# A narrow matmul tail cut into 32-column tiles, one row tile's statistics moved from VectorE to ScalarE, and the order of tasks retuned

## The chip, the cores and the metric

The kernel runs on one core of a Trainium2 chip. The metric is the device time of one execution in microseconds, the median of several. Each run is labelled fast or slow, from its time and its granted clock.

## The reference, cut to what matters

One transformer layer's work on x of 2048 rows by 512, in bf16: a layernorm, then attention and a gated feed-forward network on the same normalised rows, both added to x.

```python
xn = _layernorm(x, axis=-1)                      # mean, variance, eps 1e-5, no scale or bias
return x + _A_ref(xn, A_wqkv, A_wo) + _B_ref(xn, B_w_gate, B_w_up, B_w_down)
# _A_ref: 32 heads of 16; each row attends to 8 rows, 2 apart; softmax; output projection
# _B_ref: (gelu(xn @ w_gate) * (xn @ w_up)) @ w_down, inner width 1376
```

## The kernel before: the parts that the change touches

The program is a list of tasks with inputs, outputs, a cost and a priority. A list scheduler orders them for each of five engines, from the costs, the priorities and a table of corrections called SHIFT. Each engine's program is then its list in that order, with semaphore waits between engines. So a change of one task can move tasks elsewhere.

The inner width of 1376 is ten tiles of 128 and a rest of 96. The last 64 columns of w_up, "the up tail", have no full-width matmul to go with. They run at the head of the task that sums the attention logits, whose matmuls are 32 columns wide, four side by side on TensorE:

```python
for kt in range(4):
    for c in range(2):                                   # the up tail: two tiles of 64 columns
        ins = e.matmul(PS[64 * c:64 * c + 64, 512 * itu.slot:512 * itu.slot + 256],
                       lhsT=Wt[:, kt, 128:192],
                       rhs=xnT[:, itx.slot, kt, 256 * c:256 * c + 256],
                       start=(kt == 0), stop=(kt == 3), tile_position=(0, 64 * c))
for (g, prs) in grp:
    for wq in range(2):
        for sj in range(4):                              # the logits: four tiles of 32 columns
            ins = e.matmul(PS[32 * sj:32 * sj + 32, ...], lhsT=E8[:, 24 - 8 * g:56 - 8 * g], ...,
                           tile_position=(0, 32 * sj))
```

There are four such tasks, one per 512 rows. The attention output uses 32-wide matmuls too (weights E4). In two of the four places such an output block lies right before the task; so there are six narrow blocks in all.

The layernorm's statistics were made by VectorE for every row tile of 128 rows, and the start of the program has a fixed order on each engine ("chain"):

```python
t_of["bnst%d" % t] = G.task("dve", ..., lambda e: e.bn_stats(out=st[:, t, :], in_=XIN[:, it.slot, t2, :]), ...)
t_of["bnag%d" % t] = G.task("dve", ..., lambda e: e.bn_aggr(out=mv[:, t, :], in_=st[:, t, :]), ...)
# ... cut ...
chain(["bnst0", "bnag0", "sub0", "rstd0", "norm0", "bnst1", "bnag1", "evy0_0", "sub1", "rstd1", "norm1", ...
```

## Time and profile before

| | before |
|---|---|
| time, median of 6 runs | 195.23 us (195.07 to 195.54) |
| profiled span | 193.5 us |
| TensorE busy | 97% of the span |
| Q weights landed | 6.13 us |
| first projection on TensorE starts | 6.26 us |
| last matmul starts | 190.78 us |

The three views (the page's totals and chain, TensorE's waits, the timeline of one narrow block) are shown and read in the prediction. One more is needed to follow the second row tile. These are lines of the timeline of the kernel before; the columns are start and length in us, engine, line, operation, output and inputs, their sizes, the count, and in brackets the idle time before and what ended it:

```profile
4.75 0.69 DVE L937 BATCH_NORM_STATS2 st<-XIN 128x6 f32<-128x512 bf16 x1
...
5.38 0.38 ACT L1039 ACTIVATE xnT<-PS 128x256 bf16<-128x256 bf16 x1 [1.13 <-PE PS L1019]
...
6.21 0.35 DVE L993 TENSOR_SCALAR XIN<-XIN,rstd 128x512 bf16<-128x512 bf16 x1
...
6.26 0.61 PE L1077 MATMUL PS<-xnT,Wqkv 128*128 128x128 bf16 x8 [0.65 <-DVE rstd L969]
...
6.71 0.39 PE L1019 MATMUL PS<-ident,XIN 128*128 128x128 bf16 x4
```

VectorE takes the second tile's statistics at 4.75 and has it normalised at 6.56. ScalarE evacuates the first tile's transposes until 5.76. TensorE waits 0.65 us, then multiplies the first tile with the Q weights at 6.26, and turns to the second tile's transposes at 6.71, when that tile has been ready for 0.15 us.

### The profile page before, as it was taken

To read this page: it belongs to the slowest core of one execution; us is meant where nothing else is said; L and a number is where in the kernel's file an instruction comes from. 1 tells how busy PE (TensorE), PEld (TensorE's weight loads), DVE (VectorE), ACT (ScalarE), POOL (GpSimd) and SP (SyncE) were. 2 spreads that over 40 slices of the span, in tenths; PEclk is the share of its full clock that TensorE was granted. 3 is DMA by queue.
4 is the path that set the end of the run, shared out by engine and by line. 5 is a ranking of instruction groups with operands and counts; after the bars stand their busy time and mean duration, and the time that the engine had idled before them with its cause. 6 is when DMAs were issued, how large, how long until landed. Compare 5 with 4: busy or idle time off the path is not lost.

```text
span 193.5 us, 3221 instructions
## 1 busy us (share of the span) xinstructions
PE 187.4 (97%) x1207; PEld 91.6 (47%) x1224; DVE 153.2 (79%) x241; ACT 104.0 (54%) x171; POOL 16.2 (8%) x31
## 2 busy tenths in 40 slices
PE   6899999999999999999999999999999999999994
PEld 2794444444444444444444444444444444444484
DVE  5898999999998988995895699988997089931132
ACT  3587583996676665501667777328266640048000
POOL 6013001014711000000200000000000000000000
DMA  5999999898375006953511587420250298130121
GB/s 134 354 396 305 327 168 178 216 277 186 71 181 106 2 3 160 234 156 105 181 36 50 140 216 157 130 77 0 68 128 21 62 243 189 54 112 0 44 79 41
DMA packets 34800, 27.03 MB, mean 140 GB/s; under 512 B 11265, under 2 KB 33249, under 8 KB 34785
## 3 DMA queue, kind: packets, MB, share of 16 engines
q1 hardware_dynamic: 34784, 26.83, 54.6%
q8 instruction: 9, 0.15, 0.3%
q14 instruction: 7, 0.05, 0.1%
HBM read 19.99 MB, written 5.26 MB: 131 GB/s over the span
## 4 chain that ended last, share of the span: by engine, by line
PE 93%; ACT 2%; DVE 2%; DMA 1%; issue 1%; DVEq 0%
PE PS L1374 34%; PE PS L1453 20%; PE PS L1131 18%; PE PS L1449 7%; PE PS L1077 4%; PE PS L1342 4%; PE PS L1215 4%; PE PS L1409 1%; PE PS L1208 1%; DMA XIN<-in_A_x_dram 1%; ACT OT L1354 1%; DVE st L937 1%; PE PS L1019 0%; ACT UU L1391 0%; DVE XIN L976 0%
## 5 line engine op out<-in xcount | busy, mean ns | idle before, releaser
L1453 PE MATMUL PS<-Wd,HT 128*128 128x512 bf16 (+2 forms) x207 | 41.2, 345 | 0.1
L1374 PE MATMUL PS<-xnT,Wu 128*128 128x512 bf16 x157 | 39.9, 379 | 0.3 <-issue 0.2
L1374 PE MATMUL PS<-xnT,Wg 128*128 128x512 bf16 x154 | 39.3, 379 | 0.7 <-issue 0.5
L1185 DVE TENSOR_TENSOR UNI<-QT,KT 128x2048 bf16<-128x2048 bf16 x32 | 37.2, 1221 | 2.3 <-PE PS L1342 1.5
L1384 ACT ACTIVATE GG<-PS 128x512 bf16<-128x512 f32 x40 | 23.8, 601 | 26.5 <-PE PS L1374 23.1
L1131 PE MATMUL PS<-xnT,Wqkv 128*128 128x512 bf16 x156 | 34.8, 379 | 0.3 <-issue 0.2
L1391 ACT ACTIVATE UU<-PS 128x512 bf16<-128x512 f32 x40 | 24.0, 599 | 15.6 <-PE PS L1374 15.6
L1396 DVE TENSOR_TENSOR HT<-GG,UU 128x512 bf16<-128x512 bf16 x40 | 16.2, 418 | 17.3 <-ACT UU L1391 17.1
L1453 PEld LDWEIGHTS PS<-Wd,HT 128*128 128x128 bf16 x209 | 19.6, 98 | 18.6
L1374 PEld LDWEIGHTS PS<-xnT,Wg 128*128 128x128 bf16 x160 | 15.4, 98 | 19.4 <-issue 0.8
L1374 PEld LDWEIGHTS PS<-xnT,Wu 128*128 128x128 bf16 x160 | 15.5, 98 | 19.3 <-issue 0.8
L1131 PEld LDWEIGHTS PS<-xnT,Wqkv 128*128 128x128 bf16 x160 | 15.5, 98 | 18.8 <-ACT OT L1354 0.4
L1473 DVE TENSOR_TENSOR OB<-PS,XR 128x512 bf16<-128x512 f32 (+2 forms) x19 | 11.4, 602 | 11.8 <-PE PS L1453 11.6
L1322 DVE TENSOR_TENSOR UNI<-BS,PT 128x2048 bf16<-128x2048 bf16 x16 | 19.5, 1219 | 0.6 <-DMA PT<-pt_scratch 0.5
L1322 DVE TENSOR_TENSOR BS<-BS,PT 128x2048 bf16<-128x2048 bf16 x16 | 19.6, 1222 | 0.3
L1449 PE MATMUL PS<-Wo,OT 128*128 128x512 bf16 (+2 forms) x75 | 16.7, 345 | 0.1
L1148 ACT ACTIVATE KT<-PS 128x512 bf16<-128x512 f32 x12 | 7.3, 606 | 14.3 <-PE PS L1131 14.3
L1155 ACT ACTIVATE VT<-PS 128x512 bf16<-128x512 f32 x16 | 9.6, 597 | 4.4 <-PE PS L1131 4.4
L937 DVE BATCH_NORM_STATS2 st<-XIN 128x6 f32<-128x512 bf16 x16 | 10.7, 685 | 1.0 <-DMA XIN<-in_A_x_dram 1.0
L1171 POOL COPY KT<-KT 128x64 bf16<-128x64 bf16 x3 | 7.6, 2518 | 40.0 <-ACT KT L1148 38.6
L1354 ACT ACTIVATE OT<-PS 128x512 bf16<-128x512 f32 x16 | 8.3, 602 | 4.3 <-PE PS L1342 4.3
L1449 PEld LDWEIGHTS PS<-Wo,OT 128*128 128x128 bf16 x76 | 7.2, 98 | 7.0
(66 smaller groups left out, 150.3 us busy)
## 6 DMA issues: line engine op xcount, KB each, us to landing
BS<-vt_scratch SPq DMA_DIRECT2D x64, 128.5 KB, 3.5
vt_scratch<-VT SPq DMA_DIRECT2D x16, 128.0 KB
XR<-in_A_x_dram SPq DMA_DIRECT2D x16, 128.0 KB, 2.2
out_dram<-OB SPq DMA_DIRECT2D x14, 128.0 KB, 2.1
Wqkv<-in_A_wqkv_dram SPq DMA_DIRECT2D x3, 512.0 KB
XIN<-in_A_x_dram SPq DMA_DIRECT2D x6, 256.0 KB, 5.8
Wg<-in_B_w_gate_dram SPq DMA_DIRECT2D x1, 1280.0 KB
Wu<-in_B_w_up_dram SPq DMA_DIRECT2D x1, 1280.0 KB
```

Source lines behind the costliest of these rows:

```text
L937: return lambda e: e.bn_stats(out=st[:, t, :], in_=XIN[:, it.slot, t2, :])
L1131: ins = e.matmul(PS[:, 512 * it.slot:512 * it.slot + HWD], lhsT=lhsT, rhs=xnT[:, itx.slot, kt, c0:c0 + HWD], start=(kt == 0), stop=(kt == 3))
L1185: return lambda e: e.tensor_tensor(out=UNI[:, it.slot, :, :], in0=bass.AP(QT, (itq.slot * 4 + g) * 512, [[NQT * 4 * 512, 128], [0, 4], [1, ...
L1322: return lambda e: e.tensor_tensor(out=dst(), in0=bass.AP(BS, it.slot * 4 * 514 + o, [[NBS * 4 * 514, 128], [514, 4], [128, 4], [1, 128]]) ...
L1354: return lambda e: e.activation(out=OT[:, ito.slot, dq, :], in_=PS[:, 512 * it.slot:512 * it.slot + 512], func=ACTF.Identity)
L1374: ins = e.matmul(PS[0:M, 512 * it.slot:512 * it.slot + 512], lhsT=Wx[:, kt, j * 128:j * 128 + M], rhs=xnT[:, itx.slot, kt, :], start=(kt = ...
L1384: return lambda e: e.activation(out=GG[0:M, ito.slot, :], in_=PS[0:M, 512 * it.slot:512 * it.slot + 512], func=ACTF.Gelu_apprx_tanh)
L1391: return lambda e: e.activation(out=UU[0:M, ito.slot, :], in_=PS[0:M, 512 * it.slot:512 * it.slot + 512], func=ACTF.Identity)
L1396: return lambda e: e.tensor_tensor(out=HT[0:M, ito.slot, j, :], in0=GG[0:M, ig.slot, :], in1=UU[0:M, iu.slot, :], op=ALU.mult)
L1449: ins = e.matmul(PS[:, 512 * it.slot:512 * it.slot + CW], lhsT=OT[:, ito.slot, dq, ti * 128:(ti + 1) * 128], rhs=Wo[:, dq, c0:c1], start=( ...
L1453: ins = e.matmul(PS[:, 512 * it.slot:512 * it.slot + CW], lhsT=HT[:, ith.slot, j, ti * 128:(ti + 1) * 128], rhs=Wd[:, j, c0:c1], start=Fal ...
L1473: return lambda e: e.tensor_tensor(out=OB[:, ito.slot, 0:CW], in0=PS[:, 512 * it.slot:512 * it.slot + CW], in1=XR[:, itx.slot, c0:c1], op= ...
```

## The change

The intent of the three parts: fewer changes of matmul width on TensorE; VectorE relieved of one row tile's statistics at the crowded start; and the SHIFT table tuned again.

```diff
 SHIFT = {
-    "acc0": 223, "acc1": 3251, "er1": 857, "er2": 1563, "er3": -682, ...      # (cut: 5 lines)
+    "acc1": 4275, "er1": 814, "er2": 3235, "er3": -369, "fin0": 704, ...      # (cut: 4 lines)
 }
...
+                if t == 1:
+                    for (nm, dur, kw, rd, wr) in (
+                            ("sx1", 0.55, dict(out=junk[:, :], func=ACTF.Identity, accum_out=sums[:, 0:1]), ...),
+                            ("negm1", 0.2, dict(out=sums[:, 1:2], in_=sums[:, 0:1], func=ACTF.Identity,
+                                                scale=-1.0 / D), ...),
+                            ("sxx1", 0.55, dict(out=junk[:, :], func=ACTF.Square, bias=sums[:, 1:2],
+                                                accum_out=sums[:, 2:3]), ...),
+                            ("var1", 0.2, dict(out=mv[:, 1, 1:2], in_=sums[:, 2:3], func=ACTF.Identity,
+                                               scale=1.0 / D), ...)):
+                        ... # four ScalarE tasks
+                    t_of["mean1"] = G.task("dve", "mean1", 0.1, ...)           # mean = sum / D
+                    continue
...
-        chain(["bnst0", "bnag0", "sub0", "rstd0", "norm0", "bnst1", "bnag1", "evy0_0", "sub1", "rstd1", "norm1",
+        chain(["bnst0", "bnag0", "sub0", "rstd0", "norm0", "mean1", "sub1", "evy0_0", "rstd1", "norm1",
...
-                chain(["evx0_0", "sq1", "evx0_1", "evq0_0", "sq2"])
+                chain(["sx1", "sq0", "negm1", "sxx1", "var1", "sq1", "evx0_0", "evx0_1", "evq0_0", "sq2"])
...
-                            for c in range(2):
-                                ins = e.matmul(PS[64 * c:64 * c + 64, 512 * itu.slot:512 * itu.slot + 256],
-                                               lhsT=Wt[:, kt, 128:192],
-                                               rhs=xnT[:, itx.slot, kt, 256 * c:256 * c + 256],
-                                               start=(kt == 0), stop=(kt == 3), tile_position=(0, 64 * c))
+                            for c in range(4):
+                                ins = e.matmul(PS[32 * c:32 * c + 32, 512 * itu.slot:512 * itu.slot + 256],
+                                               lhsT=Wt[:, kt, 128 + 32 * (c % 2):160 + 32 * (c % 2)],
+                                               rhs=xnT[:, itx.slot, kt, 256 * (c // 2):256 * (c // 2) + 256],
+                                               start=(kt == 0), stop=(kt == 3), tile_position=(0, 32 * c))
```

## The prediction

> **What bounds the kernel now.** I read the page's first and fourth parts, then TensorE's own waits, then the timeline around one narrow-tile block, then the start of the chain.
>
> ```profile
> PE 187.4 (97%) x1207; PEld 91.6 (47%) x1224; DVE 153.2 (79%) x241; ACT 104.0 (54%) x171; POOL 16.2 (8%) x31
> ...
> PE 93%; ACT 2%; DVE 2%; DMA 1%; issue 1%; DVEq 0%
> ```
>
> TensorE is busy for 97% of the 193.5 us span, and 93% of the chain that ended last is TensorE. A busy matmul engine is not always a full one, so the next view lists everything TensorE waited for:
>
> ```profile
> PE PS L863 <- DVE wsrc L812: 1.5, 1, 1.5
> PE PS L1077 <- DVE rstd L969: 0.7, 1, 0.7
> PE PS L1374 <- issue: 0.6, 4, 0.2
> PE PS L1131 <- issue: 0.2, 1, 0.2
> ```
>
> The first two are before 6.26 us; after that nothing is waited for except "issue". I went through the starts of consecutive matmuls in the trace. A full 128x512 one follows the last at 0.2157 us without exception, but for two things: about a dozen steps of exactly twice that, which are lost records (17 of the full-width matmuls that the program has are missing from the trace, and a lost record after a narrow block also makes the "0.16 issue" below), and the changes of tile width. One real wait is left after 6.26: 0.19 us at 7.37, for the second row tile's evacuation. So from 6.26 to 191.04 TensorE is full, and the time moves only by (a) what TensorE itself has to do, (b) its start, (c) the 2.4 us tail, (d) stalls that a new order brings.
>
> For (a), the block in which the up tail lies:
>
> ```profile
> 72.79 0.39 PE L1342 MATMUL PS<-BS,E 128*32 128x512 bf16 x4
> 73.11 0.63 PE L1208 MATMUL PS<-xnT,Wt 128*64 128x256 bf16 x8
> 73.67 1.91 PE L1215 MATMUL PS<-UNI,E 128*32 128x512 bf16 x32
> 75.73 0.59 PE L1131 MATMUL PS<-xnT,Wqkv 128*128 128x512 bf16 x2 [0.16 <-issue]
> ```
>
> Columns: start, length, engine, line, tiles, weights' shape, moving shape, count. The four 32-wide matmuls at 72.79 stream together for 0.216, to 73.00; L1208 (the up tail) starts at 73.107, so going from 32-wide to 64-wide cost 0.103. Its pairs start at 73.107, 73.240, 73.350 and 73.459; the last ends streaming at 73.568, and L1215 starts at 73.665: going back to 32-wide cost 0.097. From full width to a narrow block (28.96 to 29.05) it is 0.093.
>
> For (b), the start of the chain:
>
> ```profile
> 4.83 0.61 DVE st L937
> 5.45 0.02 issue
> 5.47 0.18 DVE mv L941
> 5.65 0.18 DVE xnT L1031
> 5.83 0.26 DVE XIN L976
> 6.09 0.10 DVE rstd L969
> 6.19 0.07 issue
> 6.26 0.61 PE PS L1077 x8
> ```
>
> This reads as if VectorE's statistics of the second row tile (st, mv at 4.83 to 5.65) held the first projection. They do not. That matmul needs the first row tile's transposes, evacuated by 5.76 (ScalarE) and 5.83 (VectorE), and the Q weights. The trace's DMA completions put the last of the 16 pieces of those weights at 6.13, TensorE's semaphore wait for them ends at 6.155 to 6.206, and its weight load starts at 6.23. The chain names the reciprocal only because it is the nearest earlier end. The start is held by a 512 KB weight load which the change leaves alone.
>
> **What the Trainium skill says.** "TensorEngine Tiling (Array Packing)", Tiling Modes, Key Properties: changing the tiling mode, not just the tile, drains TensorE, and different tiles load weights and multiply in parallel. The trace agrees: 0.093 to 0.106 us at each change of width, and four 32-wide matmuls start within 0.01 us of each other. "TensorE: Matmul & The Clock Gate", section "Wait — 56ns, not 53.3ns?": start to start is N / 2.4 GHz plus 2.5 ns when warm, so 0.109 for N = 256; the 64-wide pairs show 0.109 to 0.110. "ScalarE: Activation LUTs", What ACT_TABLE_LOAD costs: an ACTIVATE takes 186 ns + 0.833 ns per element, 93 ns more with a bias pointer, and neighbours overlap by about 93 ns. Here the 512-wide copies take 597 ns (613 by the formula) and the one-column square root with a bias pointer 297 ns (281).
>
> **The change part by part.**
> *Up tail.* Eight 64-wide matmuls of 256 columns, in concurrent pairs, become sixteen 32-wide ones, in groups of four. Streaming is the same: four steps of 0.109. What goes is changes of width, as both neighbours that are narrow are 32-wide. The change to 32-wide after the up tail goes in all four blocks: 4 x 0.097 = 0.39. The change before it goes where another 32-wide block comes right before, two of four (the lists of both programs agree on that): 2 x 0.103 = 0.21. The first pair after a change takes 0.133 in place of 0.109; this 0.024 goes in two blocks for sure: 0.05. Sum 0.65 us, all on TensorE's full stretch, so all of it counts. I take 0.6, because groups of four must have four weight loads of 97 ns done within 109 ns, with little to spare.
>
> *Second row tile.* VectorE loses bn_stats 0.685 and its aggregation 0.18 and gains a one-column multiply, about 0.16. ScalarE gains two passes over 512 columns (estimated by the skill's formula at 0.61 and 0.71, the second having a bias pointer) and two one-column operations (0.19 each). In order: the row tile's DMA lands at 3.46; sum 3.49 to 4.10; first tile's square root 4.00 to 4.30 (was 3.95); negative mean 4.21 to 4.40; squares 4.42 to 5.13; variance 5.15 to 5.35; square root 5.37 to 5.67 (was 5.69 to 5.98); evacuation of the first transposes 5.57 to 5.96 (was 5.38 to 5.76). The second tile is normalised at about 6.3 instead of 6.56, but TensorE gets to its transposes only at 6.70, behind eight matmuls that wait for the weights: gain 0. The later evacuation at 5.96 is still ahead of 6.13: loss 0, with 0.15 us to spare.
>
> *The retuned priorities.* The diff replaces the whole table, and this is its largest part in the program. The lists show the same TensorE instructions in another order, with the same six narrow blocks, so no work is gained or lost; only stalls could come. I checked the tight places. The first logits block moves up: 56 full matmuls instead of 68 after 14.49, so 14.49 + 56 x 0.2157 = 26.6. Its eight VectorE products now run without a break from about 15.5, at a step of 1.135: 15.5 + 7 x 1.135 + 1.22 = 24.7, 1.9 us ahead. The fourth logits block keeps its distance (products end 124.89, block at 126.14 now). In the trace the last product of the four output blocks ends 1.0, 2.2, 2.0 and 3.8 us ahead of its block (70.26 before 71.27, and so on). In the new order, adding up streaming times, the first of them comes at about 72.9, 1.6 us later, with about as much VectorE work ahead of its last input (one 0.42 us product less, one 0.68 us product more). The third and fourth come about 1.5 us earlier, 0.65 of it the shift that I predict; the third has one 0.42 us product less in front of its last input, whose wait for a ScalarE copy (one per 1.73 us of matmuls) goes too; the fourth had 3.8 us. At the end there are five groups instead of four between the last narrow block and the final output tiles, which cover the four evacuations (2.0 us) at least as well. The final tiles and stores are unchanged: tail 0.
>
> Sum: 195.24 - 0.6 = 194.6 us; the span goes from 193.5 to about 192.9.
>
> **Rivals.** *The chain is right and the statistics hold the start:* then about 0.25 us more would come (6.56 to 6.3): 194.4. For it speaks only the chain; against it the landing at 6.13. *ScalarE becomes the bound at the start:* if accumulating costs ScalarE 0.1 us a pass more, the evacuation ends near 6.2, the first projection slips by 0.1 to 0.2, and, as TensorE is full afterwards, the slip stays: 194.8. Nothing in the trace has an accumulating pass, so this is open. *The new order stalls TensorE:* one late product or evacuation costs some tenths to 1 us: 195 to 195.6. For it: ScalarE and VectorE orders changed everywhere; and VectorE is 94 to 96% busy from 14.5 to 75.7 and from 111 to 129 us. Against: the old order, made by the same scheduler with the same margins, had no stall with a VectorE just as full. *Sixteen short weight loads do not keep up,* say 0.15 per group instead of 0.11: 4 x 4 x 0.04 = 0.64 lost, and the gain is gone: 195.2.
>
> **Range and chances.** The main term is six changes of width, each measured; the rivals lie mostly above. The runs of before span 0.47 us. Predicted 194.6, range 194.0 to 195.4. Two per cent is 3.9 us: a gain of that size is nowhere to be had with TensorE full (faster 0.01), a loss would need several long stalls (slower 0.02), so within 2% has 0.97.
>
> **What would show it.** Right: the up tail's line shows groups of four at 0.109 us, the next block starts without 0.1 us in between, the block at 73 lasts 0.2 us less, the first projection stays at 6.2 to 6.3, and TensorE waits for nothing new. Wrong: a first projection that moves with the statistics, up tail groups at clearly over 0.11, or a named wait of TensorE after 7.6 us.

## The result, and the profile after

The changed kernel takes 194.76 us (median of 6 fast runs, 194.5 to 195.03) against 195.23. The ratio is 0.9975, with a 95% interval of 0.9962 to 0.9988. Ratios here are the mean time of one kernel's fast runs over that of the other's of the same rounds, so they are not quite the ratio of the medians quoted. The gain of about a quarter of a per cent is real, as the interval leaves out 1.

First the page's totals and its chain, of the changed kernel:

```profile
PE 186.6 (97%) x1239; PEld 92.0 (48%) x1256; DVE 152.4 (79%) x240; ACT 106.1 (55%) x177; POOL 15.7 (8%) x31
...
PE 93%; DMA 4%; issue 1%; SPq 0%; DVE 0%; DVEq 0%
```

TensorE's share is as before. In the chain VectorE's share at the start has gone, and the load of the Q weights stands there (2.3% of the span). ScalarE's 2% of before were not at the start: they lay at 152.6 to 156.2, where TensorE had a lost record. An output store at the end makes up most of the rest of the 4% of DMA. TensorE's waits, of the changed kernel (what waited for what, us in total, times, longest):

```profile
PE PS L866 <- DVE wsrc L815: 1.5, 1, 1.5
PE PS L1098 <- DMA Wqkv<-in_A_wqkv_dram: 0.7, 1, 0.7
PE PS L1395 <- issue: 0.6, 4, 0.2
PE PS L1395 <- ACT OT L1375: 0.3, 2, 0.2
```

The same 0.7 us wait that was put down to VectorE's reciprocal before is now put down to the load of the Q weights. The third and fourth lines are not waits: each is a narrow block (the 32- and 64-column matmuls between two full-width ones) followed by a full-width group with one record lost, which the block below shows (x3 where the program has four). Here 17 of the 1256 matmuls have no record, as in the trace of the kernel before (1207 of 1224), while all weight loads have theirs.

Now the timeline of the block that the prediction showed for the kernel before, in the changed one:

```profile
74.42 0.39 PE L1363 MATMUL PS<-BS,E 128*32 128x512 bf16 x4
74.64 0.61 PE L1229 MATMUL PS<-xnT,Wt 128*32 128x256 bf16 x16
75.08 1.90 PE L1236 MATMUL PS<-UNI,E 128*32 128x512 bf16 x32
77.13 0.81 PE L1395 MATMUL PS<-xnT,Wu 128*128 128x512 bf16 x3 [0.16 <-ACT OT L1375]
```

From the last output group to the up tail it is 0.22 us, which is just the group's streaming; it was 0.32. From the up tail to the logits it is 0.44, four steps of 0.11; it was 0.56. Two changes of width and the slow first pair have gone.

Last, the start in the changed kernel, the answer to the timeline shown of the kernel before:

```profile
3.40 0.63 ACT L952 ACTIVATE junk<-XIN 128x512 bf16<-128x512 bf16 x1 [1.11 <-DMA XIN<-in_A_x_dram]
...
3.93 0.19 ACT L952 ACTIVATION_READ_ACCUMULATOR junk<-XIN 128x1 f32 x1
...
4.43 0.72 ACT L952 ACTIVATE junk<-XIN,sums 128x512 bf16<-128x512 bf16 x1
...
5.06 0.19 ACT L952 ACTIVATION_READ_ACCUMULATOR junk<-XIN,sums 128x1 f32 x1
...
5.28 0.35 DVE L997 TENSOR_SCALAR XIN<-XIN,mv 128x512 bf16<-128x512 bf16 x1 [0.32 <-ACT junk L952]
...
5.72 0.36 ACT L1060 ACTIVATE xnT<-PS 128x256 bf16<-128x256 bf16 x1
...
6.04 0.35 DVE L1014 TENSOR_SCALAR XIN<-XIN,rstd 128x512 bf16<-128x512 bf16 x1
...
6.29 0.61 PE L1098 MATMUL PS<-xnT,Wqkv 128*128 128x128 bf16 x8 [0.67 <-DMA Wqkv<-in_A_wqkv_dram]
```

The second tile is normalised at 6.40 instead of 6.56. The first tile's evacuation ends at 6.08 instead of 5.76, behind the passes on ScalarE. The Q weights land at 6.15, and the first projection starts at 6.29, which is 0.03 us later than before. Two instructions that the program does not name, the reads of the accumulator, come with the two passes.

To separate start and rest I use one mark in all kernels below, the *gate*: the start of the first matmul of the second row tile's Q projection, where TensorE waits for an evacuation for the last time. From there to the start of the last matmul is the *body*.

| profiled run | gate | last matmul starts | body |
|---|---|---|---|
| before | 7.57 | 190.78 | 183.21 |
| changed | 7.60 | 190.10 | 182.50 |

The body is 0.71 us shorter; the gate is 0.03 us later; the tail after the last matmul's start is 2.7 us in both (193.5 - 190.78 and 192.8 - 190.10). All six narrow blocks account for the 0.71, measured from the end of streaming of the last full-width matmul to the first full-width matmul after the block (where that one's record is lost, its start is taken as the next one's less a step of 0.216):

| block | before | changed | difference |
|---|---|---|---|
| logits 0 alone | 2.50 | 2.38 | -0.12 |
| outputs 0 and logits 1 | 4.35 | 4.11 | -0.24 |
| outputs 1 and logits 2 | 4.35 | 4.11 | -0.24 |
| logits 3 alone | 2.51 | 2.38 | -0.12 |
| outputs 2, outputs 3 | | | 0 |

### The profile page after: what moved, and what is told of

It reads as the page before. It is cut to its first block, busy times and chain, and to the rows that moved or that the text cites. A ratio compares the mean times of both kernels' runs of the same rounds, so it can differ in the third digit from the quotient of the medians.

```text
span 192.8 us, 3283 instructions
## 1 busy us (share of the span) xinstructions
PE 186.6 (97%) x1239; PEld 92.0 (48%) x1256; DVE 152.4 (79%) x240; ACT 106.1 (55%) x177; POOL 15.7 (8%) x31
## 4 chain that ended last, share of the span: by engine, by line
PE 93%; DMA 4%; issue 1%; SPq 0%; DVE 0%; DVEq 0%
PE PS L1395 36%; PE PS L1474 18%; PE PS L1152 18%; PE PS L1470 7%; PE PS L1098 4%; PE PS L1363 4%; PE PS L1236 4%; DMA Wqkv<-in_A_wqkv_dram 2%; PE PS L1430 2%; DMA out_dram<-OB 1%; PE PS L1229 1%; SPq L923 0%; DVE OB L1494 0%; PE PS L1040 0%; DVEq L558 0%
## 5 line engine op out<-in xcount | busy, mean ns | idle before, releaser
L1152 PE MATMUL PS<-xnT,Wqkv 128*128 128x512 bf16 x156 | 35.3, 379 | 0.2
L1343 DVE TENSOR_TENSOR BS<-BS,PT 128x2048 bf16<-128x2048 bf16 x16 | 19.6, 1224 | 0.4
L940 DVE BATCH_NORM_STATS2 st<-XIN 128x6 f32<-128x512 bf16 x15 | 10.1, 686 | 0.9 <-DMA XIN<-in_A_x_dram 0.9
L1162 ACT ACTIVATE QT<-PS 128x512 bf16<-128x512 f32 x12 | 7.2, 597 | 3.1 <-PE PS L1152 3.1
```

The source lines that it names most:

```text
L940: return lambda e: e.bn_stats(out=st[:, t, :], in_=XIN[:, it.slot, t2, :])
L1152: ins = e.matmul(PS[:, 512 * it.slot:512 * it.slot + HWD], lhsT=lhsT, rhs=xnT[:, itx.slot, kt, c0:c0 + HWD], start=(kt == 0), stop=(kt == 3))
L1343: return lambda e: e.tensor_tensor(out=dst(), in0=bass.AP(BS, it.slot * 4 * 514 + o, [[NBS * 4 * 514, 128], [514, 4], [128, 4], [1, 128]]) ...
```

## The experiments

**The theory:** the up tail alone gives the whole gain, by changes of width; the statistics and the new order give nothing, as the start is held by the Q weights and TensorE never waits later. **The rivals:** the statistics hold or delay the start; or the order hides a loss or a gain of its own.

All kernels below gave correct results. Each was timed in five rounds beside the kernel before; in the three groups this had medians of 195.54, 195.36 and 195.36 us.

### One part alone, and all but one part

`u_only`: the kernel before with the 32-wide up tail only. The order of the lists is unchanged.

```diff
-                            for c in range(2):            # 64 columns each
+                            for c in range(4):            # 32 columns each, as in the change
```

> The kernel before with the up tail in 32-wide column tiles, nothing else; its program lists are otherwise the same, instruction by instruction. My theory (the whole gain is the changes of tile width saved): first projection stays near 6.26 us, the two logits blocks with full matmuls before them get 0.12 us shorter, the two after an output block 0.235 shorter, last matmul starts 0.7 us earlier, median 194.6 (ratio 0.9965). Rival 1 (the second row tile's statistics give part of it): only 0.4 to 0.5 us here. Rival 2 (the retuned order gives it): under 0.2 us here.

Measured: 194.89 us (194.43 to 195.11), ratio 0.9964 (0.9949 to 0.9978). The body is 182.50. Its trace lost no record, so its block can be read without corrections:

```profile
PE 189.2 (98%) x1256; PEld 92.9 (48%) x1256; DVE 153.2 (79%) x241; ACT 103.9 (54%) x171; POOL 16.3 (8%) x31
...
73.08 0.39 PE L1342 MATMUL PS<-BS,E 128*32 128x512 bf16 x4
73.29 0.61 PE L1208 MATMUL PS<-xnT,Wt 128*32 128x256 bf16 x16
73.73 1.90 PE L1215 MATMUL PS<-UNI,E 128*32 128x512 bf16 x32
75.56 1.90 PE L1131 MATMUL PS<-xnT,Wqkv 128*128 128x512 bf16 x8
```

The 32 logits matmuls, eight groups of 0.2157, stream for 1.73 us, and 75.56 - 73.73 is 1.83. So going back to full width costs 0.106 (from the unrounded starts), and the 0.16 us of idle time that the traces with lost records show at this place does not exist. One part of the change has the whole effect on the body.

`no_u`: the changed kernel with the 64-wide up tail.

```diff
-                            for c in range(4):
+                            for c in range(2):            # 64 columns each, as before
```

> The changed kernel with the up tail back in 64-wide tiles. My theory: 195.2 to 195.3 (ratio 1.000), the last matmul at 190.8 as before. If statistics or order gave a part, that part is still here: faster than before by 0.2 us or more.

Measured: 195.21 us (195.13 to 195.54), ratio 0.9988 (0.9976 to 1.0001); body 183.21. Statistics and new order together are not told apart from nothing.

`s_only`: the kernel before with the new SHIFT table only.

```diff
-    "acc0": 223, "acc1": 3251, "er1": 857, ...           # the old table
+    "acc1": 4275, "er1": 814, "er2": 3235, ...           # the new one
```

> The kernel before with the new table of priorities alone. My theory: same TensorE work in another order, no new stall, so 195.2 (ratio 1.000 +- 0.001), last matmul within 0.1 us of 190.78. Rival 2 (the order brings the gain): 0.3 us or more faster. Rival 3 (the order costs something that the up tail pays for): 0.2 us or more slower.

Measured: 195.24 us (195.05 to 195.62), ratio 0.9991 (0.9975 to 1.0006); body 183.21, the same to 0.001 us. The new order has no stall and no gain. Its profiled run shows something else, by chance: the Q weights landed at 5.83 there, 0.3 us earlier than in the kernel before. Its timeline:

```profile
5.96 0.61 PE L1076 MATMUL PS<-xnT,Wqkv 128*128 128x128 bf16 x8 [0.31 <-DMA Wqkv<-in_A_wqkv_dram]
...
6.22 0.35 DVE L992 TENSOR_SCALAR XIN<-XIN,rstd 128x512 bf16<-128x512 bf16 x1
...
6.63 0.40 PE L1018 MATMUL PS<-ident,XIN 128*128 128x128 bf16 x4
```

The first eight matmuls were done streaming at about 6.4, and then TensorE waited 0.22 us for the second tile, which VectorE had normalised at 6.57. The gate came at 7.50, only 0.07 us earlier. So when the weights come early, VectorE's statistics do bind. When they come at 6.13 they do not. How much of the 0.22 us the ScalarE statistics could win back is another question, as they delay the first tile; `n_x` and `a_x` below answer it.

`no_l`: the changed kernel with VectorE's statistics, new table and 32-wide up tail kept. TensorE's list is that of the changed kernel.

```diff
-                if t == 1:                                # the four ScalarE tasks and mean1
-        chain(["bnst0", "bnag0", "sub0", "rstd0", "norm0", "mean1", "sub1", "evy0_0", "rstd1", "norm1",
+        chain(["bnst0", "bnag0", "sub0", "rstd0", "norm0", "bnst1", "bnag1", "evy0_0", "sub1", "rstd1", "norm1",
-                chain(["sx1", "sq0", "negm1", "sxx1", "var1", "sq1", "evx0_0", "evx0_1", "evq0_0", "sq2"])
+                chain(["evx0_0", "sq1", "evx0_1", "evq0_0", "sq2"])
```

> The changed kernel with the second row tile's statistics back on VectorE; TensorE's list is the same as in the changed kernel. My theory: as fast as the changed kernel (194.6 to 194.8, ratio 0.9972), first projection at 6.26 to 6.29 because the Q weights land at 6.13 to 6.16. Rival 1 (statistics on ScalarE help): slower than the changed kernel by 0.2 us or more, the first projection or the second row tile's transposes later.

Measured: 195.02 us (194.69 to 195.54), ratio 0.9978 (0.9963 to 0.9993); body 182.50. The changed kernel itself has 0.9975: taking the ScalarE statistics out changes nothing that can be measured, with intervals of 0.3 us to either side.

`l_only`: the kernel before with the ScalarE statistics only; old table, 64-wide up tail.

```diff
+                if t == 1:                                # the four ScalarE tasks and mean1
-        chain(["bnst0", "bnag0", "sub0", "rstd0", "norm0", "bnst1", ...
+        chain(["bnst0", "bnag0", "sub0", "rstd0", "norm0", "mean1", ...
```

> The kernel before with the second row tile's statistics on ScalarE alone (old table, old up tail; the schedule puts some matmuls in another order). My theory: 183.21 us from the gate to the last matmul as in every kernel with the old up tail, the start where the Q weights put it (first projection 0.10 to 0.15 after they land), so ratio 0.998 to 1.001. If the statistics alone are worth 0.2 us or more: 0.998 or less.

Measured: a clear miss. Five runs took 210.08 to 211.48 us (ratio 1.0786, 1.076 to 1.0812) at a granted clock of 0.967 to 0.975, and one, the profiled one, took 714.51 us. In that one, the step from one 512-column matmul to the next is mostly 0.840 us instead of 0.2157, from the third matmul to the end, so TensorE ran at about a quarter of its speed (0.2157 / 0.840 = 0.26), while the page gives its clock as 1.0. Nothing can be read from that time. But its order can be read, and so can the waits that even so slow a TensorE had:

```profile
PE PS L1471 <- ACT OT L1376: 5.0, 2, 2.8
...
PE PS L1364 <- DVE BS L1344: 3.5, 1, 3.5
```

In this program, the scheduler put the output projection (L1471) of the third and the fourth 512 rows directly behind the narrow blocks that make its inputs (L1364), with nothing in between; the kernel before has four matmul groups between the last block and its projection, the changed one five. So TensorE waits for four evacuations of 0.6 us each, twice, and 3.5 us before the third block. With the old table, the new tasks upset the order of the whole program, presumably because it was tuned for another set of tasks. How much of the 15 us is these waits, and how much is the lower clock in the five runs, stays open, as no full-speed run was profiled. So `l_only` does not measure the statistics; the pairs of the changed kernel with `no_l`, and of `no_u` with `s_only`, do.

### The changed kernel once more

`after_again`: the changed kernel, unedited, on another chip than the runs above.

```diff
 (no edit)
```

> The changed kernel once more, beside the next three on one chip. From the first four runs: from the first projection of the second row tile (the last gate of the start) to the last matmul TensorE takes 182.50 us with the new up tail and 183.21 with the old one, to 0.002 us in every trace. Expected again: 182.50 here, ratio 0.9970 +- 0.0012.

Measured: 194.58 us (194.42 to 195.34), ratio 0.9972 (0.9955 to 0.9989); gate 7.58, body 182.50. This trace lost no record and shows no wait after the gate.

### Can the start be had earlier?

If the Q weights hold the start, bringing them earlier should help, and the ScalarE statistics should then be worth something.

`b_w`: the kernel before, with the Q weights' load issued from ScalarE's queue at the very start, instead of third on SyncE's. `a_w`: the changed kernel with the same edit.

```diff
             t_w = G.task("sp", "ld_w" + nm, 0, mk(), wr=[(I_wq, nm)], ...)
+            t_w.on_act = nm == "q"
```

> The kernel before with the 512 KB load of the Q weights issued from ScalarE's queue at the start, so that it lands earlier; all lists of compute instructions as before. If the weights hold the start, the first projection moves from 6.26 to about 5.95 (the first row tile's evacuation ends at 5.83), and then the second row tile's normalising (6.56) becomes the bound: its transposes at about 6.63 and the gate at about 7.49 instead of 7.57. Total 0.1 us faster at most. If the statistics hold the start already, nothing moves.

> The changed kernel with the same early load. First projection at about 6.15 (the evacuation ends at 6.08 here), transposes of the second row tile at about 6.6, gate at about 7.46 instead of 7.60; 0.13 us faster than the changed kernel. So with the weights early the statistics on ScalarE would be worth only some hundredths against the gate of the kernel before with early weights.

Measured: both slower, though within 2% (the intervals leave out 1), and so misses. `b_w` took 195.96 us (195.78 to 196.31), ratio 1.0033 (1.0021 to 1.0045); `a_w` took 197.44 (196.48 to 197.98), ratio 1.0096 (1.0073 to 1.0119). The timeline of `b_w`:

```profile
5.96 0.69 DVE L938 BATCH_NORM_STATS2 st<-XIN 128x6 f32<-128x512 bf16 x1 [0.71 <-DMA XIN<-in_A_x_dram]
...
6.78 0.26 DVE L1032 COPY xnT<-PS 128x256 bf16<-128x256 bf16 x1
...
7.14 0.61 PE L1078 MATMUL PS<-xnT,Wqkv 128*128 128x128 bf16 x8 [1.17 <-issue]
```

The weights did land earlier, at 5.60 instead of 6.13. But the second row tile, 128 KB, landed at 5.93 instead of 3.46, since now 512 KB moved beside it. VectorE's list has that tile's statistics before the copy of the first tile's transposes, so the copy came at 6.78, and the first projection at 7.14. The gate is 8.71, the body 183.21 as before: the whole loss lies in the start. In the changed kernel the same late tile hits a worse place:

```profile
5.57 0.63 ACT L953 ACTIVATE junk<-XIN 128x512 bf16<-128x512 bf16 x1 [2.81 <-DMA XIN<-in_A_x_dram]
...
6.51 0.17 DVE L991 RECIPROCAL rstd<-sq 128x1 f32<-128x1 bf16 x1 [1.95 <-ACT sq L973]
```

ScalarE's list has the second tile's first pass ahead of the first tile's square root. So the first tile, which had its variance at 4.16, waited for the second to land. That is a price of the change that its own trace does not show: it makes the first tile depend on the second one's arrival. The gate of `a_w` came at 10.41, another 1.7 us behind that of `b_w`: after an idle stretch of 1.9 us before the first transposes at 7.12, TensorE went on at half its rate, with steps of 0.107 us, until 10.7.

`a_wf`: `a_w` with the variance's own step taken out, as the square root can scale its input.

```diff
-                            ("var1", 0.2, dict(out=mv[:, 1, 1:2], in_=sums[:, 2:3], func=ACTF.Identity, scale=1.0 / D), ...
+                    if t == 1:
+                        return lambda e: e.activation(out=sq[:, 1:2], in_=sums[:, 2:3], func=ACTF.Sqrt,
+                                                      scale=1.0 / D, bias=eps[:, 0:1])
```

> The same with the variance folded into the square root (scale and bias of that operation), one ScalarE operation less on the second row tile's way. ScalarE is 0.24 us earlier from there: evacuation ends at 5.84, first projection at about 5.92, normalised at 6.15, transposes at 6.37, gate at about 7.23; 0.3 us faster than the changed kernel, the fastest so far (194.4). If the gate does not move, something other than statistics and Q weights holds the start.

Measured: 197.84 us (196.27 to 198.95), ratio 1.0124 (1.0093 to 1.0155). A miss for the same cause: the second tile landed at 5.47.

The next three leave the weights where they are and issue only the second row tile's load from ScalarE's queue, which lets the loads behind it on SyncE's queue start one issue (0.5 us) earlier. `n_x` is `no_l` with this, `a_x` the changed kernel with this, and `a_xf` is `a_x` with the variance folded into the square root.

```diff
                     t_x = G.task("sp", "ld_x%d_%d" % (p, t2), 0, mk_ld(), wr=[(it_x, t2)], ...)
+                    t_x.on_act = (p, t2) == (0, 1)
```

> New table, new up tail, statistics on VectorE, and the second row tile's 128 KB load issued from ScalarE's queue, so that the Q weights behind it are issued 0.4 us earlier without passing it. Expected: both row tiles land at about 3.0 to 3.1, the Q weights at about 5.7 to 5.9; first projection 5.95; now the second row tile, normalised on VectorE at about 6.56, holds its transposes at 6.63 and the gate at 7.49. 0.1 us faster than the changed kernel.

> The changed kernel with the same two loads. Statistics on ScalarE start 0.3 us earlier; evacuation of the first row tile at about 6.0, first projection 6.1, second row tile normalised at 6.33, transposes at 6.55, gate at 7.42: 0.07 us ahead of the run with VectorE's statistics. If instead the ScalarE passes are in the way of the first tile, the first projection is later than 6.2 and it is slower than that run.

> The same, with the variance folded into the square root (one ScalarE operation less). Evacuation at about 5.8, first projection 5.9, transposes of the second tile at 6.35, gate at 7.21, if the Q weights are there by 5.8: 0.2 us ahead of the previous run, 0.35 us ahead of the changed kernel, ratio to the kernel before 0.9950.

| | time, us | ratio (95%) | Q weights landed | first projection | gate |
|---|---|---|---|---|---|
| `n_x` | 195.17 (194.9 to 195.49) | 0.9987 (0.9974 to 1.0001) | 5.25 | 6.34 | 7.91 |
| `a_x` | 195.21 (194.75 to 195.61) | 0.9989 (0.9974 to 1.0003) | 5.42 | 6.54 | 7.86 |
| `a_xf` | 194.76 (194.58 to 195.08) | 0.9969 (0.9954 to 0.9983) | 6.30 | 6.56 | 7.87 |

In `n_x` and `a_x` the weights landed 0.7 to 0.9 us earlier, as hoped, and the gate came later all the same. The first row tile's load now has the second one's issued beside it at the same moment: in `n_x` it landed at 3.39 instead of 2.98, and the tile was normalised from 4.89 on instead of 4.48. In `a_x` ScalarE's passes then stood in the way of the first projection. TensorE's waits of `a_x`:

```profile
PE PS L1099 <- ACT xnT L1061: 0.5, 1, 0.5
PE PS L1041 <- DVE mv L956: 0.5, 1, 0.5
```

The first line is the evacuation by ScalarE, which ended at 6.48. This is the rival of the prediction in which ScalarE holds the start, brought about by earlier weights. But the gate of `a_x` is no later than that of `n_x`: in `n_x`, whose first projection is 0.20 us earlier, TensorE then waits for the second tile, which VectorE has normalised at 6.98 against 6.80. So with early weights the ScalarE statistics moved the gate by 0.05 us, and the times, 195.21 against 195.17, do not tell the two apart. In `a_xf` the weights landed late, at 6.30, so its trace does not show what the folded variance is worth. It is no better than the changed kernel, whose ratios are 0.9975 and 0.9972. So no version with an edited load beats the change; and `u_only`, at 0.9964, is as good as the whole of it.

### What the runs scatter by

The bodies of eleven traces (all but `l_only`, and `a_w` and `a_wf`, in which TensorE's steps were still doubled beyond the gate; `after_again` counts as a trace of its own) lie within 0.002 us of 183.21 or of 182.50, by the width of their up tail. What differs from run to run is the start: without any edit of the loads, the Q weights landed anywhere from 5.71 (`no_l`) to 6.43 (`no_u`), and in some runs TensorE had not come up to its full rate. The first projection of `u_only`:

```profile
6.11 1.04 PE L1077 MATMUL PS<-xnT,Wqkv 128*128 128x128 bf16 x8
```

Eight matmuls take 1.04 us with a step of 0.107, against 0.61 and 0.056 in the kernel before; the gate came at 7.98 although the weights had landed at 5.93. (What the Trainium skill says of this is in the last section.) A median over six runs of a kernel carries a few tenths of this scatter. That is the likely reason (each run's start was not traced) that the times show gains between 0.0022 (`no_l`) and 0.0036 (`u_only`) of the time where the bodies show one and the same 0.71 us (0.0036 of 195.4).

## Why the prediction was right, point by point

**TensorE full from 6.26 on: right.** The body is the same to 0.002 us in all kernels with the same up tail, ten kernels with two different orders. The reading of the "0.16 issue" waits as lost records was confirmed by the eight traces without lost records, in which they are gone.

**The up tail: the mechanism was right, the size a little low.** Summed to 0.65 and taken as 0.6, it measured 0.71. The mis-sized term is the slow first step after a change: its 0.024 was counted in two blocks and goes in all four, which makes the sum 0.70. A block alone lost 0.12, which is the 0.097 of the change and the 0.024 of the first step. The two double blocks lost 0.235 each (`no_u` and `u_only`, no records lost), where 0.097, 0.103 and 0.024 make 0.224. The rest is in the traces too: the first 32-wide step after a change takes 0.226 instead of 0.216. These 0.010 go in the double blocks; alone, the block keeps them, as it still has one change (its first up tail step is 0.119). With them the sum is 0.71. The rounding down to 0.6, for fear that short weight loads would not keep up, was not needed: the groups of four go at 0.109.

**The second row tile: no gain and no loss, right for the starts that were seen, by a smaller margin than said.** The landing of the Q weights holds the first projection in both. The evacuation was predicted to end at 5.96 and ended at 6.08, so the spare time before the weights' landing at 6.15 was 0.07 us and not 0.15. What was left out is the instruction that reads the accumulator, 0.19 us after each pass: from the start of a pass to that of the next task it took 0.12 us more than predicted, twice. That the evacuation slipped by 0.12 and not by more is luck: the second tile landed at 3.37 instead of the 3.46 of before. In `no_u`, with the same start, it landed at 3.48 and the evacuation ended at 6.18; only there the weights came at 6.43. The rival "ScalarE becomes the bound" named just that size and just missed coming true; `a_x` shows it come true for the first projection. The second tile was ready at 6.40 instead of the predicted 6.3, because its square root ended at 5.81 instead of 5.67. Also left out, but nearly free here: the subtraction writes over what the second pass reads, so VectorE waited 0.32 us for ScalarE at 5.28; its copy after that ended at 5.83, 0.02 us after the square root that its next task needs. And the rival "the statistics hold the start" is not wrong in every run: with early weights `s_only` waited 0.22 us for the second tile. But moving the statistics to ScalarE brought only 0.05 us of gate in the pair with early weights, `n_x` and `a_x`.

**The retuned table: 0, right.** `s_only` has the body of the kernel before to 0.001 us, and in the changed kernel the first output block came at 72.90, where 72.9 was predicted. What the prediction did not see is why the diff has a new table: with the old one, the new ScalarE tasks lead the scheduler to an order that stalls, as the list and the waits of `l_only` show.

**The tail: 0, right**, 2.7 us in both.

**The whole:** 194.6 predicted, 194.76 and 194.58 measured in two sets of runs. That it comes so close is in part luck: the medians fell by 0.47 and 0.78 us, and the starts scatter by as much as the two differ. The 0.71 of the bodies is the figure to trust.

## What to carry to other kernels

When an engine is full, count what it does besides its work: here six changes of matmul width were the whole gain, and neighbours of equal width made them needless. Before you speed up a chain at the start, find what lands last there, and remember what `b_w` and `a_w` showed: the load brought forward made the one beside it 2.5 us late, and the late input held up what stood behind it in an engine's list. When a diff brings its own retuned order, test the parts with that order, since a part in a foreign order measures the order.

## What the Trainium skill lacked or had wrong

- "TensorEngine Tiling (Array Packing)", Key Properties, says that a change of tiling mode drains TensorE but gives no size. Here it is 0.093 us from 128 to 32 columns, 0.097 from 64 to 32, 0.103 from 32 to 64 and 0.106 from 32 to 128, and in the first step after a change 0.024 more at 64 columns and 0.010 more at 32.
- "ScalarE: Activation LUTs" says that an ACTIVATE can give an accumulator output, and does not say what this costs. Here each such pass brings a separate instruction of 187 ns that reads the accumulator, about 0.1 us of it exposed. The passes themselves took 631 and 722 ns, where its formula for an ACTIVATE (section "What ACT_TABLE_LOAD costs") gives 613 and 706.
- "TensorE: Matmul & The Clock Gate", section "What's actually happening", says that the array runs at half speed until about 3.4 us of activity have been seen, in windows that do not start with the kernel, so that the moment varies by 500 ns to either side. `u_only` agrees on the half speed, with steps of 0.107 us instead of 0.056. The moment varied more: with the first matmul at 1.51 us in all, full steps began at 4.3 us in `no_u` and at 7.3 us in `u_only` (TensorE was not busy throughout, so this is no clean test). Its section "Seeing it yourself" warns that the clock gate has been seen stuck at a quarter for over 50 us. Here one execution of `l_only` ran at about a quarter for nearly all of its 713 us, with steps of mostly 0.840 us, and its recorded clock said 1.0.
- No page that I read has a size for what a load costs its neighbours at a program's start; it would belong to "DMA: Bandwidth & Descriptors". In `b_w`, 512 KB on a second queue brought a 128 KB tile from 3.46 to 5.93 us, and came only 0.53 us earlier itself.
